# Four more of layer one's output-weight chunks in split form in the first token group

## The chip, the cores and the metric

One core of a Trainium2 chip. The metric is the device time of one execution, in microseconds (us); the number quoted for a kernel is the median of its runs. Engines are named as in the profile: PE (matmul) with PEld (its weight loads), DVE (vector), ACT (scalar), POOL (gpsimd), SP (here only the queue that issues transfers).

## What is computed

Causal block attention, then two feed-forward layers, all in float32 (4 batches, 8 heads, 576 positions, head size 64; so 2304 tokens of 512 features):

```python
attn = softmax(mask(q @ k.T / 8)) @ v            # block-causal, blocks of 64
x = attn as [2304, 512]
h = x @ w_in                                     # layer one: 512 -> 2048
x = (h - tanh(h)) @ w_out                        #            2048 -> 512
xn = x / sqrt(mean(x * x) + 1e-6) * rms_g        # layer two
out = (silu(xn @ w_gate) * (xn @ w_val)) @ w_out2
```

## The kernel before

Tokens are worked in six groups of 384 (three tiles of 128). The hidden 2048 features of layer one are 16 chunks of 128 (`J1`); a step `s` is one chunk of one group, so layer one is 96 steps, group 0 being steps 0 to 15. In a step, PE multiplies the chunk's input weights with the group's tokens (`ins`, L796 to L798), ACT takes the tanh (L1058), DVE subtracts it, and two steps later (`LAG`) `out1` multiplies the result with the chunk's output weights into three accumulators `acc`. Attention for the coming group runs in slots between these products, and PE's order is the order in which the program is written. The order on DVE, ACT, POOL and SP is made by a scheduler that goes by its own estimate of the times.

A float32 product is made in one of two forms:

- **split**: both factors are rounded to a shorter float (`h`) and a rest (`l`), and three fast matmuls are summed (L829 to L831 in `gemm_out`). The weights then take a whole tile of 128x1024, `h` in the left half and `l` in the right.
- **whole**: one matmul on plain float32 (L839). PE runs it as two recorded instructions. Two chunks share a tile.

Output weights of the chunks under `SPLIT` are whole in group 0, all others split. In group 0 the weights come from the inputs as 64-bit floats, staged through three buffers `st` by SP (L139) and turned into float32 by `convert`: two ACT passes (L150, L152) and two DVE passes (L153, L154). Where the result is to be split, ACT rounds it (L113, `w<-cv`) and DVE takes the rest (L117, `w<-cv,w`). The tiles of four slots for output weights are reused in turn, and what later groups need is stored to HBM: the input weights split (`w1d_i`, L730), split output weights split (`w1d_o`, L736), whole ones as pairs (`w1f`, L745). In group 1, which walks the chunks backwards, the whole ones come back through `st` (`stagef`, L756), are split by ACT and DVE (L769, L770) and stored split (L771); later groups load them split (L775).

The lines that the number decides:

```python
            if j >= SPLIT:
                t = wo[j] = wo[until(j)] = w1tile(1, until(j))
                convert(staged.pop(n), t[:, 0:512], t[:, 512:1024])
                if j < KEPT:
                    SP.dma_start(out=w1d[1][j], in_=t.bitcast(F32))
                return
...
            if s < SPLIT:
                gh = wk.tile([128, TG], F32, name="gh", tag="gh", bufs=3)
                DVE.tensor_tensor(gh, h, gt, ALU.subtract)
            else:
                DVE.tensor_tensor(gt, h, gt, ALU.subtract)
                gh = wk.tile([128, TG], F32R, name="gh", tag="gh", bufs=3)
                gl = wk.tile([128, TG], F32R, name="gl", tag="gl", bufs=3)
                rnd(ACT, gh, gt)
                lo(DVE, gl, gt, gh)
```

The weights of layer two are converted by the same `convert` during the last group of layer one and, for chunks 3 to 9, while layer two is already running over its first pair of groups (`direct`, `fill`: ACT L884 and L892, DVE L117 `ws<-fu,ws`).

Of the kernel before, what the change touches and what calls it, by code (L numbers as in the profile page):

```python
# [50 lines left out]
JH = J2 // 2  # L51
WHOLE = range(3, 10)
LAG = 2
SPLIT = 8
KEPT = 12
AVLEAD = 3

# [47 lines left out]
def build(ctx, tc, q, k, v, w_in, w_out, w_gate, w_val, w_out2, rms_g, ident_in, out):  # L105
# [566 lines left out]
    with tc.manual_schedule(engines={PE.engine}):  # L672
# [39 lines left out]
        def w1tile(x, last, dt=F32R):  # L712

            n = min(range(4), key=lambda n: lastuse[x][n])
            lastuse[x][n] = last
            return ring.tile([128, 1024], dt, name=f"w1{x}{n}", tag=f"w1{x}{n}")

        def until(s):
            g, j = divmod(s, J1)
            return s + 2 * (J1 - 1 - j) + 1 if g < NG - 1 and j >= J1 - 4 else s  # L720

        def convert1(n):

            j, half = divmod(n, 2)
            if half == 0:
# [5 lines left out]
# [3 lines that stand above are left out]
# [19 lines left out]
        def stagef(m):  # L753
            if m >= 0:
                fstaged[m] = env["stg"].tile([128, 1024], F32, name="st", tag="st")
                SP.dma_start(out=fstaged[m], in_=w1f[m])  # L756

        def w1get(s):
# [7 lines left out]
            t = wo[s] = w1tile(1, until(s))  # L766
            if g == 1 and j < SPLIT:
                f = fstaged[j // 2][:, 512 * (j % 2):512 * (j % 2) + 512]
# [12 lines left out]
        def conv_upto(m):  # L781
            nonlocal ncv
            while ncv < min(m, 2 * J1):
                convert1(ncv)
                ncv += 1
                stage1(ncv + 2)
# [46 lines left out]
        def out1(s, t):  # L833
# [3 lines left out]
            gh, gl = gts[s]  # L837
            if s < SPLIT:
                PE.matmul(accs[t], lhsT=gh[:, t * 128:t * 128 + 128], rhs=wo[s], start=(j == 0), stop=(j == J1 - 1))  # L839
# [172 lines left out]
        for s in range(NSA):  # L1012
# [26 lines left out]
            if g == 0:  # L1039
                conv_upto(max(2 * j + 3, EARLY + (2 * J1 - EARLY) * (2 * j + 1) // 28))  # L1040
            if 0 <= s - (J1 - 1 + KEPT - SPLIT) < 3:
                stagef(SPLIT // 2 - 1 - (s - (J1 - 1 + KEPT - SPLIT)))
            if KEPT <= 2 * J1 - 2 - s < J1:
# [15 lines left out]
            gl = None  # L1059
            if s < SPLIT:  # L1060
                gh = wk.tile([128, TG], F32, name="gh", tag="gh", bufs=3)
# [351 lines left out]
```

## Time and profile before

| what | value |
|---|---|
| median of 3 runs | 1007.89 us (1007.11 to 1009.34) |
| the profiled execution | 1006.96 us |
| its span, first to last instruction | 1005.1 us |
| PE, DVE, ACT, POOL busy | 994.3, 712.9, 660.0, 367.1 us |
| granted PE clock | 0.999 |

The profiled execution's time is 1.86 us above its span, and 0.93 us under the median of the runs. PE is at work in nearly all of the span; the engines that feed it have idle time when averaged over the whole, though not in each stretch.

### The profile page before, as it was taken

The numbers are of one execution on the slowest core, as the hardware profiler recorded it, in microseconds if no ns is written. First come the engines' busy times: TensorE is split into PE (matmuls) and PEld (weight loads), VectorE is DVE, ScalarE is ACT, GpSimd is POOL, SyncE is SP. The second block draws the span as 40 slices with busy tenths as digits, with TensorE's granted clock in tenths as the row PEclk, the third lists the DMA queues.
The fourth block names the chain that finished last, engine by engine and source line by source line (L and its number), as shares of the span: only waits on it lengthen the run. The fifth ranks groups of instructions, "written<-read, shape, count | busy, mean of one in ns | idle before, by whom it ended". The sixth has DMA issues, their size and how long they took to land.

```text
span 1005.1 us, 18056 instructions
## 1 busy us (share of the span) xinstructions
PE 994.3 (99%) x5987; PEld 910.9 (91%) x5987; DVE 712.9 (71%) x1577; ACT 660.0 (66%) x1546; POOL 367.1 (37%) x556
## 2 busy tenths in 40 slices
PE   9999999999999999999999999999999999999998
PEld 6767889899988889889999889999999999999998
DVE  7878876876767686787767888966854458644565
ACT  7979988887888777788858775635722247412253
POOL 6522212342334343535424524575211470111710
PEclk9999999999999999999999999999999999999999
DMA  9999889955888699767879998977796757876664
GB/s 226 293 346 353 221 267 288 253 149 141 209 241 208 196 251 296 213 211 243 284 247 383 354 360 318 349 301 301 273 350 235 265 210 269 303 275 234 261 229 149
DMA packets 185419, 265.22 MB, mean 264 GB/s; under 512 B 109040, under 2 KB 150384, under 8 KB 178032
## 3 DMA queue, kind: packets, MB, share of 16 engines
q1 hardware_dynamic: 184240, 263.69, 80.8%
q8 instruction: 47, 0.77, 0.3%
q10 hardware_dynamic: 1088, 0.39, 0.1%
q14 instruction: 44, 0.36, 0.1%
HBM read 202.70 MB, written 61.34 MB: 263 GB/s over the span
## 4 chain that ended last, share of the span: by engine, by line
PE 80%; DVE 7%; ACT 6%; DMA 4%; issue 2%; POOL 1%; DVEq 0%; SPq 0%; ACTq 0%; POOLq 0%
PE t L796 5%; PE t L798 5%; PE t L797 5%; PE acc L829 5%; PE acc L831 5%; PE acc L830 5%; PE gv L1146 5%; PE gv L1148 5%; PE gv L1147 5%; PE t L603 4%; PE t L533 4%; PE ga L831 3%; PE ga L1148 3%; PE ga L829 3%; PE ga L830 3%; PE ga L1146 3%
## 5 line engine op out<-in xcount | busy, mean ns | idle before, releaser
L796 PE MATMUL t<-xh,w 128*128 128x384 f32 x384 | 138.9, 362 | 0.0
L798 PE MATMUL t<-xh,w 128*128 128x384 f32 x384 | 129.9, 338 | 0.1
L797 PE MATMUL t<-xl,w 128*128 128x384 f32 x384 | 129.2, 337 | 0.0
L1146 PE MATMUL gv<-xh,ws 128*128 128x384 f32 x330 | 111.0, 336 | 0.5 <-DVE vb L1199 0.5
L1148 PE MATMUL gv<-xh,ws 128*128 128x384 f32 x330 | 110.9, 336 | 0.2 <-DVE ws L117 0.2
L1147 PE MATMUL gv<-xl,ws 128*128 128x384 f32 x330 | 110.7, 335 | 0.0
L829 PE MATMUL acc<-w,gh 128*128 128x512 f32 x264 | 109.2, 414 | 0.6 <-ACT gh L113 0.6
L831 PE MATMUL acc<-w,gl 128*128 128x512 f32 x264 | 104.4, 396 | 0.1
L830 PE MATMUL acc<-w,gh 128*128 128x512 f32 x264 | 103.9, 393 | 0.0
L1203 POOL TENSOR_TENSOR g<-va,vb 128x384 f32<-128x384 f32 x36 | 37.3, 1037 | 163.0 <-ACT va L1202 147.3
L574 ACT ACTIVATE pt<-pt,stat 128x64 f32<-128x64 f32 (+2 forms) x144 | 81.2, 564 | 16.4 <-DVE pt L572 11.3
L796 PEld LDWEIGHTS t<-xh,w 128*128 128x128 f32 x384 | 72.3, 188 | 6.9 <-issue 3.2
L797 PEld LDWEIGHTS t<-xl,w 128*128 128x128 f32 x384 | 72.5, 189 | 2.0 <-issue 0.5
L798 PEld LDWEIGHTS t<-xh,w 128*128 128x128 f32 x384 | 72.1, 188 | 0.8 <-DVE w L117 0.8
L117 DVE TENSOR_TENSOR gl<-gt,gh 128x384 fp32r<-128x384 f32 x88 | 60.1, 683 | 16.5 <-ACT gh L113 15.7
L117 DVE TENSOR_TENSOR pp<-t,pp 128x512 fp32r<-128x512 f32 (+3 forms) x112 | 55.4, 508 | 22.5 <-ACT pp L113 22.1
L1064 DVE TENSOR_TENSOR gt<-t,gt 128x384 f32<-128x384 f32 x88 | 48.5, 552 | 28.2 <-ACT gt L1058 27.8
L603 PE MATMUL t<-ident,pt 128*128 128x128 f32 x400 | 64.8, 274 | 0.5 <-POOL pt L588 0.5
L113 ACT ACTIVATE pp<-t 128x512 fp32r<-128x512 f32 (+5 forms) x144 | 60.5, 438 | 5.7 <-PE t L603 4.5
L1146 PEld LDWEIGHTS gv<-xh,ws 128*128 128x128 f32 x330 | 61.9, 188 | 1.4 <-DVE vb L1199 1.2
L1148 PEld LDWEIGHTS gv<-xh,ws 128*128 128x128 f32 x330 | 61.9, 188 | 0.6 <-DVE ws L117 0.6
L603 PEld LDWEIGHTS t<-ident,pt 128*128 128x128 f32 x400 | 49.9, 140 | 13.6 <-issue 3.0
(225 smaller groups left out, 2946.3 us busy)
## 6 DMA issues: line engine op xcount, KB each, us to landing
ws<-w2d SPq DMA_DIRECT2D x26, 1792.0 KB, 7.4
ws<-wod SPq DMA_DIRECT2D x21, 1536.0 KB, 6.2
w<-w1d_i SPq DMA_DIRECT2D x60, 512.0 KB, 4.8
w<-w1d_o SPq DMA_DIRECT2D x52, 512.0 KB, 5.4
w2d<-ws SPq DMA_DIRECT2D x10, 1792.0 KB, 8.5
st<-in_moe_w_out SPq DMA_DIRECT2D x28, 512.0 KB, 5.9
st<-in_moe_w_in SPq DMA_DIRECT2D x16, 512.0 KB, 6.1
w1d_i<-w SPq DMA_DIRECT2D x16, 512.0 KB, 5.3
```

The lines of the kernel that those rows point to most:

```text
L117: eng.tensor_tensor(out=o, in0=full, in1=hi.bitcast(F32), op=ALU.subtract)
L574: ACT.activation(out=pt[:, 0:keys], in_=pt[:, 0:keys], func=AF.Exp, scale=-1.0, bias=least, accum_out=st[:, 8 + ti:9 + ti])
L603: PE.transpose(t[:, (j - a) * 128:(j - a + 1) * 128], pt[:, j * 128:(j + 1) * 128], ident)
L796: PE.matmul(h, lhsT=wh[:, c], rhs=xh[:, kk], start=(kk == 0), stop=False)
L797: PE.matmul(h, lhsT=wh[:, c], rhs=xl[:, kk], start=False, stop=False)
L798: PE.matmul(h, lhsT=wl[:, c], rhs=xh[:, kk], start=False, stop=(kk == KD - 1))
L829: PE.matmul(acc, lhsT=gh[:, c], rhs=wh, start=first, stop=False, skip_group_check=more)
L830: PE.matmul(acc, lhsT=gh[:, c], rhs=wl, start=False, stop=False, skip_group_check=more)
L831: PE.matmul(acc, lhsT=gl[:, c], rhs=wh, start=False, stop=last, skip_group_check=more)
L1146: PE.matmul(ps, lhsT=wh[:, c], rhs=xh[:, kk], start=(first and kk == 0), stop=False, skip_group_check=more)
L1147: PE.matmul(ps, lhsT=wh[:, c], rhs=xl[:, kk], start=False, stop=False, skip_group_check=more)
L1148: PE.matmul(ps, lhsT=wl[:, c], rhs=xh[:, kk], start=False, stop=(last and kk == nk - 1), skip_group_check=more)
```

## The change

```diff
 WHOLE = range(3, 10)
 LAG = 2
-SPLIT = 8
+SPLIT = 4
 KEPT = 12
 AVLEAD = 3
```

For chunks 4 to 7 (steps 4 to 7 of group 0) the output weights are now split when they are converted, the tanh result is split too, the product is three matmuls in place of one whole one, and each chunk is stored split in `w1d_o` rather than in pairs in `w1f`. In group 1 these four chunks are loaded split; their splitting and storing there is gone, and two loads of `w1f` remain in place of four.

PE's order changes only in the twelve products themselves. On the other engines the scheduler's order moves in two stretches: from the conversion of chunk 4 to the start of group 1, and from the last two steps of layer one through the conversions under layer two. Three places follow.

SP in group 0, the queue that issues stores of converted weights and loads of the next raw ones; the number behind a name tells tiles apart, w1d_i_90 is the input weights of chunk 5, w1d_o_105 to w1d_o_107 the output weights of chunks 4 to 6, w1f_66 the pair of chunks 4 and 5. Before:

```order
L139 DMA st<-in_moe_w_out 128x1024
L310 DMA qr<-in_q 96x2x256
L139 DMA st<-in_moe_w_in 128x4x256
L745 DMA w1f_66<-w_887 128x1024
L730 DMA w1d_i_90<-w_922 128x1024
L139 DMA st<-in_moe_w_out 128x1024
L730 DMA w1d_i_91<-w_1010 128x1024
L139 DMA st<-in_moe_w_in 128x4x256
L139 DMA st<-in_moe_w_out 128x1024
```

The same place now:

```order
L736 DMA w1d_o_105<-w_887 128x1024
L139 DMA st<-in_moe_w_out 128x1024
L310 DMA qr<-in_q 96x2x256
L139 DMA st<-in_moe_w_in 128x4x256
L730 DMA w1d_i_90<-w_925 128x1024
L736 DMA w1d_o_106<-w_969 128x1024
L139 DMA st<-in_moe_w_out 128x1024
L730 DMA w1d_i_91<-w_1016 128x1024
L139 DMA st<-in_moe_w_in 128x4x256
L139 DMA st<-in_moe_w_out 128x1024
L736 DMA w1d_o_107<-w_1039 128x1024
```

Every chunk now has a store of its own, two of them directly ahead of a load of raw weights.

DVE around step 6, from one row maximum of the attention scores (L572, 384 columns) to the next (64 columns, the next unit's first); w_1033 is the whole tile of chunks 6 and 7, w_1136 the input weights of chunk 8. Before:

```order
L572 TENSOR_SCALAR pt,stat<-t 128x384
L153 TENSOR_SCALAR cv<-cv 128x512
L154 SCALAR_TENSOR_TENSOR w_1033<-cv,cu 128x512
L583 RECIPROCAL stat<-stat 128x3
L1062 TENSOR_TENSOR gh<-t,gt 128x384
L153 TENSOR_SCALAR cv<-cv 128x512
L154 SCALAR_TENSOR_TENSOR cv<-cv,cu 128x512
L117 TENSOR_TENSOR w_1136<-cv,w_1136 128x512
L572 TENSOR_SCALAR pt,stat<-t 128x64
```

The same place now (w_1039 and w_1108 are the split output weights of chunks 6 and 7, w_1089 the input weights of chunk 7):

```order
L572 TENSOR_SCALAR pt,stat<-t 128x384
L154 SCALAR_TENSOR_TENSOR cv<-cv,cu 128x512
L117 TENSOR_TENSOR w_1039<-cv,w_1039 128x512
L117 TENSOR_TENSOR gl<-gt,gh 128x384
L117 TENSOR_TENSOR w_1089<-cv,w_1089 128x512
L583 RECIPROCAL stat<-stat 128x3
L153 TENSOR_SCALAR cv<-cv 128x512
L154 SCALAR_TENSOR_TENSOR cv<-cv,cu 128x512
L1064 TENSOR_TENSOR gt<-t,gt 128x384
L117 TENSOR_TENSOR w_1108<-cv,w_1108 128x512
L117 TENSOR_TENSOR gl<-gt,gh 128x384
L572 TENSOR_SCALAR pt,stat<-t 128x64
```

The 64-column maximum now stands behind a `w` rest and a `gl`, where it stood behind a `w` rest alone; the rest for chunk 8's input weights has moved behind it.

ACT at the end of layer one, from the split of step 94's result to the first copy of layer two (L1195). Before:

```order
L113 ACTIVATE gh<-gt 128x384
L1058 ACTIVATE gt<-t 128x384
L150 ACTIVATE cv<-st 128x512
L152 ACTIVATE cu<-st 128x512
L113 ACTIVATE gh<-gt 128x384
L846 ACTIVATE sq,ssq<-acc_7191 128x512
L846 ACTIVATE sq,ssq<-acc_7195 128x512
L846 ACTIVATE sq,ssq<-acc_7199 128x512
L150 ACTIVATE cv<-st 128x512
L152 ACTIVATE cu<-st 128x512
```

The same place now:

```order
L113 ACTIVATE gh<-gt 128x384
L150 ACTIVATE cv<-st 128x512
L152 ACTIVATE cu<-st 128x512
L1058 ACTIVATE gt<-t 128x384
L113 ACTIVATE gh<-gt 128x384
L846 ACTIVATE sq,ssq<-acc_7227 128x512
L150 ACTIVATE cv<-st 128x512
L152 ACTIVATE cu<-st 128x512
L846 ACTIVATE sq,ssq<-acc_7231 128x512
L846 ACTIVATE sq,ssq<-acc_7235 128x512
L150 ACTIVATE cv<-st 128x512
L152 ACTIVATE cu<-st 128x512
```

The last tanh of layer one has moved behind a pair of conversion passes, and from here on the conversions run one piece (half a chunk's weights) further ahead than before.

## Rows read from the trace of the kernel before

**Rows 1.** The page: span, and busy time of each engine.

```profile
span 1005.1 us, 18056 instructions
PE 994.3 (99%) x5987; PEld 910.9 (91%) x5987; DVE 712.9 (71%) x1577; ACT 660.0 (66%) x1546; POOL 367.1 (37%) x556
```

**Rows 2.** Busy time by stretch: PE, PEld, DVE, ACT, POOL, clock, DMA, GB/s.

```profile
60.00:70.00 10.00, 10.00 (x40) 6.58 (x39) 7.16 (x18) 7.98 (x22) 1.71 (x4) 1.00 1.06 364
...
80.00:90.00 10.00, 10.00 (x45) 6.79 (x42) 8.54 (x20) 9.01 (x25) 0.15 (x1) 1.00 1.04 325
...
110.00:120.00 10.00, 10.00 (x56) 9.18 (x57) 8.48 (x23) 9.93 (x27) 0.15 (x1) 1.00 0.72 188
...
180.00:190.00 10.00, 10.00 (x61) 8.89 (x60) 8.00 (x20) 8.55 (x20) 4.46 (x6) 1.00 0.92 259
```

**Rows 3.** PE in order of time: start, us, what, idle time before it.

```profile
72.72 2.74 PE L839 MATMUL acc<-w,gh 128*128 128x512 f32 x6
75.30 0.33 PE L533 MATMUL t<-kh,qf 128*128 128x64 f32 x2
...
78.84 1.41 PE L657 MATMUL t<-pp,vp 128*64 128x384 f32 x10 [1.16 <-DVE pt L572]
...
134.30 0.39 PE L829 MATMUL acc<-w,gh 128*128 128x512 f32 x1
...
134.98 0.31 PE L533 MATMUL t<-kh,qh 128*128 128x320 f32 x1
```

**Rows 4.** The chain that ended last, from 48 to 80 us: start, us, what.

```profile
60.38 7.46 DMA st<-in_moe_w_in
...
77.11 0.64 ACT w L113
...
78.57 0.23 DVE pt L572 x2
...
78.84 1.29 PE t L657 x7
```

**Rows 5.** Groups of instructions, 40 to 100 us: count, busy us, mean ns.

```profile
L117 DVE TENSOR_TENSOR w<-cv,w 128x512 fp32r<-128x512 f32 x14 | 10.0, 716 | 2.2 <-ACT w L113 2.0
L154 DVE SCALAR_TENSOR_TENSOR cv<-cv,cu 128x512 int32<-128x512 int32 x14 | 10.0, 714 | 1.4 <-ACT cu L152 0.2
L113 ACT ACTIVATE w<-cv 128x512 fp32r<-128x512 f32 x14 | 9.0, 643 | 0.9 <-DVE cv L154 0.8
...
L117 DVE TENSOR_TENSOR gl<-gt,gh 128x384 fp32r<-128x384 f32 x2 | 1.1, 551 | 0.0
L113 ACT ACTIVATE gh<-gt 128x384 fp32r<-128x384 f32 x2 | 1.1, 528 | 0.0
```

**Rows 6.** Transfers from 40 to 100 us: rate by slices of 1.5 us, total, issues.

```profile
GB/s 143 139 370 407 358 426 336 253 391 419 341 333 261 325 401 283 283 398 420 410 390 397 333 155 304 420 380 244 337 263 302 372 414 382 401 416 399 410 373 313
DMA packets 11907, 20.55 MB, mean 343 GB/s; under 512 B 2266, under 2 KB 8572, under 8 KB 11902
...
w1f<-w SPq DMA_DIRECT2D x4, 512.0 KB, 5.4
w1d_o<-w SPq DMA_DIRECT2D x3, 512.0 KB, 6.0
```

**Rows 7.** Busy time by stretch under layer two's first conversions, columns as above.

```profile
630.00:640.00 10.00, 9.69 (x56) 9.63 (x56) 9.36 (x19) 6.05 (x13) 4.55 (x5) 1.00 0.98 353
...
650.00:660.00 10.00, 9.62 (x53) 8.98 (x52) 9.58 (x18) 4.76 (x11) 4.58 (x5) 1.00 0.55 229
660.00:670.00 10.00, 9.19 (x50) 8.22 (x50) 6.45 (x12) 3.15 (x7) 8.62 (x10) 1.00 1.01 390
```

**Rows 8.** ACT in order of time at the end of layer one.

```profile
589.57 0.66 ACT L150 ACTIVATE cv<-st 128x512 f32<-128x512 f32 x1
590.13 0.67 ACT L152 ACTIVATE cu<-st 128x512 int32<-128x512 uint32 x1
590.69 0.53 ACT L113 ACTIVATE gh<-gt 128x384 fp32r<-128x384 f32 x1
```

## The prediction

> **What bounds the kernel now.** The first view is the page: PE is busy for 994.3 of 1005.1 us, so all idle time of PE together is under 11 us, and a change is worth what it does to PE's work or to these few gaps [rows 1]. The second is busy time by stretch, for the part of group 0 that is changed, roughly 55 to 96 us. PE shows 10.00 of 10 both at 60 to 70 and at 80 to 90, with DVE at 7.16 and 8.54 and ACT at 7.98 and 9.01 [rows 2]. So PE sets the pace there, but ACT has little room. The third is PE in order of time. The one large gap near the change is 1.16 us before 78.84, where the value product of attention waits for DVE [rows 3]. The fourth is the chain that ended last, which tells where that wait comes from: a raw-weight load issued at 60.38 that took 7.46 us, then ACT and DVE passes of the conversion, a rounding at 77.11, and the row maximum (L572) at 78.57, which stood in DVE's queue behind the weights' rest [rows 4]. What the reader is to see: up to 78.84 the end is set by loads, ACT and DVE, and from there on by PE. A saving on PE counts in full behind that gap; ahead of it it only makes the gap longer.
>
> **PE's own work.** Three whole products (six records) run from 72.72 to the next start at 75.30, so one takes 2.58 / 3 = 0.86 us. Three split matmuls run from 134.30 to 134.98, so a split product takes 0.68 us [rows 3]. Each of the twelve products of chunks 4 to 7 gains 0.18 us, 2.16 in all. The three of chunk 4, at 72.72, lie ahead of the gap: 0.54 us of gain that falls into it. The nine of chunks 5 to 7 lie behind it: 9 x 0.18 = **1.6 us off the end**. The PE clock is at full in all these stretches [rows 2], so the durations carry over.
>
> **Work added on ACT and DVE in group 0.** Four roundings of weights at 0.643 and four of results at 0.528 make 4.7 us on ACT; four rests at 0.716 and four at 0.551 make 5.1 us on DVE [rows 5]. The second conversion pass on DVE remains as it was, only its target changes. Spread over the 30 to 40 us of these steps that is 12 to 17% of either engine. At 60 to 70 there is room for it: 2.0 us idle on ACT and 2.8 on DVE [rows 2]. Steps that were split already run with ACT at 9.93 and DVE at 8.48 at 110 to 120 us, and PE is at 10.00 there [rows 2]. So in sum the cover holds, and I cost the added passes at nothing except where they stand directly ahead of something that PE waits for. If the cover were gone, ACT's 4.7 us would be the price, the upper end.
>
> That place is the gap at 78.84. In DVE's order the 64-column maximum stood behind one weights' rest; now it stands behind a weights' rest and a `gl`, in a stretch that also holds one more rest, one more `gl`, and the same conversion passes. The least is that the gap vanishes (1.16 us gained), since the old order's wait for the rounding at 77.11 is not the new order's wait. The most is one `gl` (0.551) plus a later load. The load of 60.38 now has one more store of 512 KB in flight ahead of it, and 524 KB at the mean 343 GB/s of 40 to 100 us is 1.5 us [rows 6]; together 2.1 us. I take **0.7 us lost**: the `gl` in full, and little of the store, because the chain is nearest to a DVE queue there and ACT had idle time that the added passes fill before the load is waited for.
>
> **Transfers.** Out go two stores of pairs (`w1f`); in come four stores (`w1d_o`) of the same 512 KB each [rows 6]. That is two more, 1.05 MB, in the 50 us after 50: 3.1 us at the mean rate of 343 GB/s if all of it delayed loads that are waited for. The slices do not stand at the mean: they swing from 139 to 426 GB/s and are at 390 or more in 16 of 40 [rows 6], so some room is left between bursts, and by 110 to 120 us the rate has fallen to 188 [rows 2], so what is late is caught up. SP issues in order, and each new store waits for its rest on DVE before the next raw load can go. I put all this inside the 0.7 above and its bound of 2.1.
>
> The Trainium skill (DMA: Bandwidth & Descriptors, "Where 436 GB/s comes from") says that for transfers between HBM and SBUF the HBM side binds at about 358 GB/s per core, and this speaks against the change: a stretch at 343 would have 4% left, and the two more stores would push loads back by nearly their whole length, an estimate of 1.05 MB / 358 = 2.9 us. The slices of up to 426 GB/s do not agree with that as a ceiling for one core running alone. By the row the sum is as above; by that rule the loss at the gap would be about 2.9 instead of 0.7, and the end 2.2 us later.
>
> **Group 1.** Four roundings, four rests and four stores go, two loads net come in. PE is at 10.00 at 180 to 190 us, with ACT at 8.55 and DVE at 8.00 [rows 2]: PE waits for none of it, so this gives nothing. The lower end would be the same nothing; a loss would need a late load of `w1d_o`, which is issued more than two steps ahead like those of the neighbouring chunks.
>
> **The end of layer one.** Here no work is changed, only the order. On ACT the last tanh moves behind a pair of conversion passes, 589.57 to 590.69, so it comes 1.1 us later [rows 8], and the last products wait for its split: up to 1.1 us lost on PE at about 592. In return the conversions under layer two run one piece ahead. In 630 to 670 PE idles 0.31 + 0.38 + 0.81 = 1.5 us with DVE at 9.36 and 9.58 of 10 [rows 7]; there DVE sets the end. One second pass (L154, 0.714 us [rows 5]) less in DVE's queue lets that stretch end 0.7 us earlier. PE by itself would end 1.1 later but has 1.5 of idle to lose, so 0.4 earlier. The later of the two decides: **0.4 us gained**, between 1.5 gained (all idle time goes) and 1.1 lost (nothing is given back).
>
> **Sum.** 1.6 gained, 0.7 lost, 0.4 gained: 1.3 us less. The profiled execution (1006.96, span 1005.1 [rows 1] and 1.86 around it) would become 1005.7. The median of the runs stands 0.93 above the profiled one, so I predict 1007.89 - 1.3 = **1006.6 us**. What a measurement of this kernel can tell from no change is about 0.2%, 2.0 us, so this is a gain within what cannot be told.
>
> **Rivals.**
> - *The savings come whole.* The gap at 78.84 stays or shrinks, chunk 4's 0.54 counts too, and layer two gives back 1.0: 2.2 + 1.0 = 3.2 less, 1004.7. For it: the idle time of ACT and DVE at 60 to 70 [rows 2], and no wait of PE at 110 to 120 under the same load. Against: the `gl` ahead of the maximum. 0.22.
> - *The gap eats the saving.* It grows by its bound of 2.1 and layer two gives 0.4: 1.6 + 0.4 - 2.1 = 0.1 less, 1007.8. For it: the chain through the 7.46 us load [rows 4]. 0.20. The skill's rule above would end beside it, 0.9 later than before.
> - *Slower: the loads fall behind.* Mechanism: SP holds each raw load behind a split store, the three buffers turn slower, and ACT stands at the head of its queue waiting for raw weights while exponentials and tanh wait behind it. Place: 60 to 95 us. Price: the full 3.1 us of the two stores and the `gl` 0.55, while the last tanh costs its 1.1: 3.65 + 1.1 - 1.6 = 3.2 more, 1011.1. It decides once PE's gaps in 55 to 96 grow by more than the 1.6 saved plus 2.0. Against: the chunks already split do not show it at 110 to 120 [rows 2], although with a lower transfer rate. 0.10.
>
> **How the numbers follow.** The forecast has 0.48, and by itself lies between 1005.2 and 1007.6: the layer-two term between its 0.4 and nothing, the gap between nothing and 1.4. Below 1005.9 (faster by over 0.2%) lie the first rival and a fifth of the forecast: 0.22 + 0.10 = 0.32. Above 1009.9 lie most of the slower rival: 0.09. The rest, 0.59, is within 0.2%. The range for 8 in 10 leaves out part of either end: 1004.2 (both gains whole and half the gap gone) to 1009.4 (the gap at 2.1, the last tanh's 1.1 not given back, and half a microsecond between runs).
>
> **What would show it.** L839 with 24 records in place of 48, and split products at 0.68 us in steps 4 to 7. The wait before the value product near 78, grown by about 0.7 and still released by L572. PE without idle from there to 100, and step 8's first product about 0.9 us earlier. A new wait of up to 1.1 us at the end of layer one, and less than 1.5 us of idle in 630 to 670. The prediction is wrong if PE shows new gaps of more than 1 us between 80 and 100, if loads of raw weights take much over 7.5 us, or if the conversions under layer two fall behind rather than ahead.

## The result and the profile after

The changed kernel takes 1013.96 us (median of 6 runs, 1012.41 to 1014.95) against 1007.67 for the kernel before (6 runs, 1007.11 to 1009.34): ratio 1.0059, 95% interval 1.0049 to 1.0069. That is **6.3 us slower**, where 1.3 us less was predicted; it lies outside the range.

The profiled execution took 1014.95, 1.0 above the median, and that of before lies 0.7 under its own, so the two traces differ by 7.7 us. Part of this is chance: at 48 us, in code that the change doesn't touch, the trace after is already 2.2 us late, and the traces of the experiments below that keep this code are 0.5 to 2.1 late there. Shifts below are differences between two points, so this cancels.

The page of the changed kernel, span and engines, answers to [rows 1]:

```profile
span 1012.8 us, 18082 instructions
...
PE 996.2 (98%) x5999; PEld 914.4 (90%) x5999; DVE 712.6 (70%) x1581; ACT 663.4 (66%) x1550; POOL 367.9 (36%) x556
```

PE is busy 1.9 us more and idle 16.6 instead of 10.8 us. Where it idles is seen in busy time by stretch of the changed kernel, columns as in [rows 2] and [rows 7]:

```profile
60.00:70.00 10.00, 10.00 (x46) 7.55 (x45) 7.49 (x19) 7.83 (x20) 2.12 (x4) 1.00 1.08 350
80.00:90.00 10.00, 10.00 (x59) 8.49 (x55) 9.11 (x24) 9.40 (x24) 1.77 (x4) 1.00 1.02 344
110.00:120.00 10.00, 8.84 (x48) 7.65 (x47) 7.84 (x19) 9.46 (x26) 0.15 (x1) 1.00 0.79 228
120.00:130.00 10.00, 7.66 (x39) 6.58 (x39) 8.11 (x19) 9.86 (x22) 0.60 (x3) 0.83 0.53 176
...
660.00:670.00 10.00, 10.00 (x59) 10.00 (x58) 9.01 (x17) 6.13 (x13) 5.89 (x8) 1.00 0.60 215
670.00:680.00 10.00, 9.32 (x54) 9.00 (x53) 4.76 (x9) 2.00 (x4) 10.00 (x11) 1.00 1.02 394
680.00:690.00 10.00, 9.05 (x52) 8.73 (x51) 4.50 (x9) 1.92 (x4) 7.83 (x8) 1.00 0.99 404
```

The stretch that the prediction watched (60 to 90) is full. The new idle time is at 110 to 130, behind the steps that were changed and in steps that were split before; at 120 to 130 the granted clock also falls. In layer two 660 to 670 is now full, as forecast, but 670 to 690 is not.

PE in order of time in the changed kernel, columns as in [rows 3]:

```profile
75.15 0.48 PE L829 MATMUL acc<-w,gh 128*128 128x512 f32 x1
...
77.31 0.33 PE L533 MATMUL t<-kh,qf 128*128 128x64 f32 x2
...
79.57 1.52 PE L657 MATMUL t<-pp,vp 128*64 128x384 f32 x12
...
108.36 0.44 PE L796 MATMUL t<-xh,w 128*128 128x384 f32 x1 [0.25 <-ACT w L113]
...
115.56 0.44 PE L796 MATMUL t<-xh,w 128*128 128x384 f32 x1 [1.05 <-ACT w L113]
...
123.67 0.44 PE L796 MATMUL t<-xh,w 128*128 128x384 f32 x1 [2.23 <-ACT w L113]
...
124.68 0.34 PE L796 MATMUL t<-xh,w 128*128 128x384 f32 x1
124.86 0.34 PE L797 MATMUL t<-xl,w 128*128 128x384 f32 x1
...
126.28 0.52 PE L797 MATMUL t<-xl,w 128*128 128x384 f32 x1
126.60 0.52 PE L798 MATMUL t<-xh,w 128*128 128x384 f32 x1
...
598.48 0.50 PE L829 MATMUL acc<-w,gh 128*128 128x512 f32 x1 [0.41 <-ACT gh L113]
...
676.85 0.45 PE L1146 MATMUL gv<-xh,ws 128*128 128x384 f32 x1 [0.68 <-DMA ws<-w2d]
...
685.39 0.45 PE L1146 MATMUL ga<-xh,ws 128*128 128x384 f32 x1 [0.95 <-DMA ws<-w2d]
```

Three split products of chunk 4 take 2.16 us (75.15 to 77.31) where whole ones took 2.58, and the gap of 1.16 us ahead of the value product is gone (79.57 has no wait). Up to 96 us the kernel gains what the change promised: the transposes that start at 57.93 and 95.98 before start at 60.51 and 95.22 after, a shift from +2.58 to -0.76, that is **3.3 us gained** (12 products at 0.18 are 2.16, and the gap 1.16). Then PE waits three times for the rounded *input* weights of chunks 12, 13 and 14, which the change doesn't touch (and once, 0.31 us, for a rest). From 95.22 to 128.61 the shift goes from -0.76 to +6.35: **7.1 us lost**. In layer two the shift falls from 6.23 (565 us) to 5.43 (664.66 before, 670.09 after), 0.8 gained, and the two waits for `ws` raise it to 7.38: 2.0 lost.

The chain that ended last in the changed kernel, from 95 to 128 us:

```profile
93.35 4.07 DMA st<-in_moe_w_out
97.44 0.20 ACT stat L582
97.64 0.55 ACT w L113
...
122.22 0.41 ACT gh L113
122.63 0.10 ACT stat L582
122.73 0.38 ACT pp L113
123.10 0.53 ACT w L113
123.65 0.70 DVE w L117
124.40 0.44 PE t L798
```

It begins with a raw-weight load and then stays on ACT and DVE; ACT is at 9.5 and 9.9 of 10 there. How late the conversions run, SP's queue shows. First its last raw loads (L139) of layer one in the kernel before, in order of time:

```profile
112.07 0.37 SPq L139 DMA_DIRECT2D st<-in_moe_w_in  x1
114.67 0.35 SPq L139 DMA_DIRECT2D st<-in_moe_w_out  x1
```

The same in the changed kernel:

```profile
117.62 0.37 SPq L139 DMA_DIRECT2D st<-in_moe_w_in  x1
120.52 0.35 SPq L139 DMA_DIRECT2D st<-in_moe_w_out  x1
```

The two are 5.5 and 5.9 us later, over 3 more than the late start explains. Such a load is issued as soon as ACT frees a buffer: in the kernel before ACT's second pass (L152) on the buffer ends at 112.05 and the load goes at 112.07, in the changed kernel at 117.60 and 117.62. So these times tell how far ACT has come.

SP's order in layer two, in the kernel before:

```profile
657.66 0.34 SPq L899 DMA_DIRECT2D w2d<-ws  x1
658.11 6.55 SPq L1166 DMA_DIRECT2D ws<-w2d  x2
665.78 0.32 SPq L899 DMA_DIRECT2D w2d<-ws  x1
```

In the changed kernel:

```profile
663.82 0.37 SPq L1166 DMA_DIRECT2D ws<-w2d  x1
669.84 0.32 SPq L899 DMA_DIRECT2D w2d<-ws  x1
670.26 0.38 SPq L1166 DMA_DIRECT2D ws<-w2d  x1
```

A store of 1.8 MB (L899) now stands between two loads of `ws`; before, both loads stood ahead of it. So there are two losses at two places. The first could come from five things: ACT's added passes, SP's order (a load held behind a store that waits for its rest), the bytes of the stores, the number of raw buffers, or the order of work on ACT and DVE, which the scheduler makes anew for each kernel.

### The profile page after: what moved, and what is told of

Read it like the earlier page. It is cut to its first block, busy times and chain, and to the rows that moved or that the text cites. A ratio compares the mean times of both kernels' runs of the same rounds, so it can differ in the third digit from the quotient of the medians.

```text
span 1012.8 us, 18082 instructions
## 1 busy us (share of the span) xinstructions
PE 996.2 (98%) x5999; PEld 914.4 (90%) x5999; DVE 712.6 (70%) x1581; ACT 663.4 (66%) x1550; POOL 367.9 (36%) x556
## 4 chain that ended last, share of the span: by engine, by line
PE 78%; DVE 7%; ACT 7%; DMA 4%; issue 2%; POOL 1%; SPq 0%; DVEq 0%; ACTq 0%; POOLq 0%
PE t L796 5%; PE t L798 5%; PE t L797 5%; PE acc L829 5%; PE gv L1146 5%; PE gv L1148 5%; PE gv L1147 5%; PE acc L831 5%; PE acc L830 5%; PE t L603 4%; PE t L533 3%; PE ga L1146 3%; PE ga L831 3%; PE ga L829 3%; PE ga L830 3%; PE ga L1148 2%
## 5 line engine op out<-in xcount | busy, mean ns | idle before, releaser
L796 PE MATMUL t<-xh,w 128*128 128x384 f32 x384 | 139.4, 363 | 3.5 <-ACT w L113 3.5
L829 PE MATMUL acc<-w,gh 128*128 128x512 f32 x276 | 115.1, 417 | 1.0 <-ACT gh L113 1.0
L831 PE MATMUL acc<-w,gl 128*128 128x512 f32 x276 | 109.2, 396 | 0.1
L830 PE MATMUL acc<-w,gh 128*128 128x512 f32 x276 | 108.7, 394 | 0.0
L574 ACT ACTIVATE pt<-pt,stat 128x64 f32<-128x64 f32 (+2 forms) x144 | 80.9, 562 | 16.0 <-DVE pt L572 10.8
L796 PEld LDWEIGHTS t<-xh,w 128*128 128x128 f32 x384 | 72.5, 189 | 11.1 <-ACT w L113 4.7
L1064 DVE TENSOR_TENSOR gt<-t,gt 128x384 f32<-128x384 f32 x92 | 50.8, 552 | 29.1 <-ACT gt L1058 28.5
L1146 PEld LDWEIGHTS gv<-xh,ws 128*128 128x128 f32 x330 | 61.9, 188 | 1.8 <-DMA ws<-w2d 1.0
L831 PEld LDWEIGHTS acc<-w,gl 128*128 128x128 f32 x276 | 51.8, 188 | 12.6 <-DVE gl L117 1.1
```

What stands on the lines that cost most here:

```text
L574: ACT.activation(out=pt[:, 0:keys], in_=pt[:, 0:keys], func=AF.Exp, scale=-1.0, bias=least, accum_out=st[:, 8 + ti:9 + ti])
L796: PE.matmul(h, lhsT=wh[:, c], rhs=xh[:, kk], start=(kk == 0), stop=False)
L829: PE.matmul(acc, lhsT=gh[:, c], rhs=wh, start=first, stop=False, skip_group_check=more)
L830: PE.matmul(acc, lhsT=gh[:, c], rhs=wl, start=False, stop=False, skip_group_check=more)
L831: PE.matmul(acc, lhsT=gl[:, c], rhs=wh, start=False, stop=last, skip_group_check=more)
L1146: PE.matmul(ps, lhsT=wh[:, c], rhs=xh[:, kk], start=(first and kk == 0), stop=False, skip_group_check=more)
```

## The experiments

Each ratio is to the kernel before on the same chip, whose median beside these runs was 1007.67 to 1008.15. "Waits" is the sum of PE's waits for rounded or rest input weights at 105 to 128 us; MB and GB/s are the transfers of 55 to 100 us.

| kernel | median us | ratio, 95% | waits | last raw load | MB, GB/s |
|---|---|---|---|---|---|
| before | 1007.67 | | 0 | 114.67 | 15.69, 349 |
| changed | 1013.96 | 1.0059 (1.0049 to 1.0069) | 3.84 | 120.52 | 16.49, 366 |
| e1_pool | 1013.48 | 1.0049 (1.0030 to 1.0067) | 3.92 | 119.37 | 16.49, 366 |
| e2_act | 1008.85 | 1.0006 (0.9995 to 1.0016) | 0 | 116.61 | 15.65, 348 |
| e3_nostore | 1010.52 | 1.0020 (1.0011 to 1.0029) | 0 | 112.91 | 15.45, 343 |
| e4_split6 | 1009.86 | 1.0020 (1.0011 to 1.0030) | 1.10 | 118.97 | 16.25, 361 |
| e6_tiny | 1009.39 | 1.0015 (1.0006 to 1.0023) | 0 | 116.44 | 14.97, 333 |
| e7_poolq | 1016.11 | 1.0074 (1.0061 to 1.0088) | 3.85 | 121.12 | 15.83, 352 |
| e8_later | 1013.75 | 1.0056 (1.0044 to 1.0069) | 3.68 | 119.24 | 16.46, 366 |
| e9_st4 | 1008.37 | 1.0002 (0.9993 to 1.0011) | 0 | 114.14 | 16.74, 372 |
| e10_b4 | 1008.12 | 0.9999 (0.9990 to 1.0007) | 0 | 112.65 | 16.94, 376 |
| e11_l2 | 1012.07 | 1.0034 (1.0021 to 1.0047) | 3.87 | 121.44 | 16.19, 360 |
| e12_both | 1006.65 | 0.9988 (0.9980 to 0.9997) | 0 | 114.31 | 16.66, 370 |
| e13_bytes | 1011.15 | 1.0033 (1.0021 to 1.0044) | 2.73 | 118.97 | 16.67, 370 |

The column to read first is the last raw load: at 116.6 or earlier PE waits for no input weights, from 118.9 on it does. It is a sign of how late ACT's conversions run, not a cause by itself.

**Is it the added passes? e1_pool, e2_act.** e1_pool is the changed kernel with its eight added roundings on POOL:

```diff
-        rnd(ACT, h, f)
+        rnd(reng or ACT, h, f)
...
+                convert(staged.pop(n), t[:, 0:512], t[:, 512:1024], POOL if j < 8 else ACT)
...
+                rnd(POOL if s < 8 else ACT, gh, gt)
```

> The changed kernel, with the eight added rounding passes (output weights and results of chunks 4 to 7) on POOL in place of ACT; same products, same transfers. If ACT's queue is what came to be the bound (theory ACT): no wait of PE for a rounded weight between 105 and 125 us, and 1006 to 1008.5 us. If the two more stores are the cause, by holding back the raw loads (theory stores): 1012 to 1014.5 us, waits as in the changed kernel.

e2_act is the kernel before with the eight ACT passes alone, to a scratch tile:

```diff
             o = t[:, 512 * (j % 2):512 * (j % 2) + 512]
             convert(staged.pop(n), o)
+            if j >= 4:
+                rnd(ACT, wk.tile([128, 512], F32R, name="dum", tag="dum", bufs=1), o)
...
                 DVE.tensor_tensor(gh, h, gt, ALU.subtract)
+                if s >= 4:
+                    rnd(ACT, wk.tile([128, 512], F32R, name="dum", tag="dum", bufs=1)[:, 0:TG], gh)
```

> The kernel before, with only the eight ACT passes added at the same places (their results go to a scratch tile that nothing reads); products whole, stores as before. Theory ACT: 2 to 5 us slower than before, 1009.7 to 1012.7 us, PE waiting for rounded input weights late in group 0. Theory stores: within 1 us of before, 1006.7 to 1008.7 us.

Both speak against it: taken off ACT, the waits are what they were (0.35, 1.07 and 2.20 us at chunks 12 to 14), and added alone, the passes cost nothing that can be measured (1008.85 is 0.15 above the interval, but its ratio can't be told from 1). That part of the prediction, "I cost the added passes at nothing", holds for ACT's passes.

**Is it the stores, and how does it grow? e3_nostore, e4_split6.** e3_nostore is the changed kernel without the four stores; later groups load chunks 8 to 11 in place of 4 to 7, which leaves four chunks' output weights out of their products. e4_split6 makes half of the change.

```diff
-                if j < KEPT:
+                if 8 <= j < KEPT:
                     SP.dma_start(out=w1d[1][j], in_=t.bitcast(F32))
...
-                SP.dma_start(out=t.bitcast(F32), in_=w1d[1][j])
+                SP.dma_start(out=t.bitcast(F32), in_=w1d[1][j + 4 if 4 <= j < 8 else j])
```

> The changed kernel without the four stores of split output weights of chunks 4 to 7 in group 0; later groups load chunks 8 to 11 in their place, so those weights are the wrong ones. 2.1 MB less is moved in group 0, 1.05 MB less than even before. Theory stores: 1006 to 1008 us. Theory ACT: 1012 to 1014.5 us, as the changed kernel, waits of PE for ACT unchanged.

```diff
-SPLIT = 8
+SPLIT = 6
```

> The change half made: chunks 6 and 7 alone are split in group 0 (the number is 6). Half of the ACT passes, half of the stores. Either theory: between the two, 1008.5 to 1011 us; if the loss were an accident of the scheduler's order and not a sum of work, it could lie anywhere from 1005 to 1014.

Without the stores the waits for weights are gone, with ACT's and DVE's added work in place. The time missed both intervals: the 1010.5 that is left holds the two waits of layer two (0.51 and 0.96 us at `ws`), of which neither theory knew. With half of the change one wait of 1.10 is left, and SP's order in layer two is that of before. So the stores carry the first loss, and it grows with their number.

**Their place or their bytes? e6_tiny, e8_later, e7_poolq, e13_bytes.** In e6_tiny the stores keep their places and waits but are 8 KB long (loads as in e3_nostore):

```diff
+                if 4 <= j < 8:
+                    SP.dma_start(out=w1d[1][j][:, 0:16], in_=t.bitcast(F32)[:, 0:16])
+                elif j < KEPT:
                     SP.dma_start(out=w1d[1][j], in_=t.bitcast(F32))
```

> This kernel is the changed one with the four stores of the output weights of chunks 4 to 7 kept at their places in SP's queue and behind the same rests on DVE, but 8 KB long in place of 512 KB; later groups load chunks 8 to 11 in place of chunks 4 to 7, which leaves out part of the computation. Theory H (SP's order: a raw load stands behind a store that is held for its rest): the waits of PE for rounded input weights at 105 to 128 us stay as in the changed kernel, 3 us or more in sum, and the time is 1012.5 to 1014.5. Theory B (the bytes: 1.05 MB more in the stretch take the loads' bandwidth): no such wait over 0.5 us, and the time is that of the kernel without the stores, 1009.5 to 1011.

In e8_later each store goes behind the next raw load, with its full length:

```diff
                 if j < KEPT:
-                    SP.dma_start(out=w1d[1][j], in_=t.bitcast(F32))
+                    later.append((j, t))
...
                 stage1(ncv + 2)
+                while later and later[0][0] <= (ncv - 3) // 2:
+                    n, w = later.pop(0)
+                    pin(SP.dma_start(out=w1d[1][n], in_=w.bitcast(F32)))
```

> The changed kernel with each store of output weights in group 0 moved behind the raw load that followed it (in SP's order two conversions later), same bytes, same queue. Theory H (SP's order): the raw loads come earlier, the waits for input weights at 105 to 128 us shrink to 1 us or less in sum, time 1009.5 to 1011.5. Theory B (the bytes): as the changed kernel, 1012.5 to 1014.5, since the bytes in the stretch are the same.

In e7_poolq the four stores leave SP's queue:

```diff
                 if j < KEPT:
-                    SP.dma_start(out=w1d[1][j], in_=t.bitcast(F32))
+                    (POOL if j < 8 else SP).dma_start(out=w1d[1][j], in_=t.bitcast(F32))
```

> The changed kernel with the same four stores of 512 KB issued from POOL's queue in place of SP's, so that no raw load stands behind them. Theory H (SP's order): the last raw loads are issued 3 us earlier, the waits for input weights at 105 to 128 us go, and the time is 1009.5 to 1011. Theory B (the bytes): waits as in the changed kernel, 1012.5 to 1014.5. A third way: POOL is held at a store until DVE has the rest, attention's scalings of pt behind it come late, and PE waits at value products between 57 and 80 us: slower than 1012 with waits for pt instead of w.

e13_bytes is the kernel before with the bytes alone (its edit also keeps SP's order in layer two as it was):

```diff
                 SP.dma_start(out=w1f[j // 2], in_=t)
+                if j in (5, 7):
+                    SP.dma_start(out=more[j // 2 - 2], in_=t)
```

> The kernel before (nothing split more, no added ACT or DVE pass) with two more 512 KB stores to HBM in group 0: the pair tiles of chunks 4 and 5 and of 6 and 7 are stored a second time behind their own stores, to places that nothing reads; SP's order in layer two is kept as before. This is the 1.05 MB that the change adds, by itself. Theory B (the bytes: DMA engines are full from 55 to 112 us and each byte more makes the last raw loads later): the last raw loads are issued 2 to 3.5 us later than in the kernel before, PE waits for rounded input weights at 105 to 128 us, and the time is 1010 to 1013. Rival E (bytes cost only together with the added ACT and DVE passes, since those make the conversions late): no such waits, 1007.5 to 1009.

All four go the same way. Same place, hardly any bytes: no wait. Same bytes at another place or from another queue: the waits stay. Bytes alone: 3.2 us slower, with no other line of the change in the kernel. PE of e13_bytes in order of time (its L800 is L796):

```profile
122.07 0.44 PE L800 MATMUL t<-xh,w 128*128 128x384 f32 x1 [2.73 <-ACT w L113]
```

SP's last raw loads in e13_bytes (its L141 is L139):

```profile
115.21 0.37 SPq L141 DMA_DIRECT2D st<-in_moe_w_in  x1
118.97 0.35 SPq L141 DMA_DIRECT2D st<-in_moe_w_out  x1
```

Its transfers from 55 to 100 us: total, then issues with their median us to landing:

```profile
DMA packets 9378, 16.67 MB, mean 370 GB/s; under 512 B 2141, under 2 KB 6506, under 8 KB 9373
...
st<-in_moe_w_in SPq DMA_DIRECT2D x7, 512.0 KB, 7.6
...
more<-w SPq DMA_DIRECT2D x2, 512.0 KB, 7.0
```

The reader is to see the same kind of wait at the same place as in the changed kernel, 122 us, more than 40 us behind the added stores. A raw load takes 7.6 us to land there and 5.5 in e6_tiny; in the kernel before and the changed one the medians are 6.5 and 6.6, so the median alone does not show it, the time of issue does. e7_poolq has no wait for `pt` and nearly the waits for weights of the changed kernel, as theory B said, but went 1.6 us past its upper end; its interval overlaps that of the changed kernel, and the 2 us between the medians were not followed up. e6_tiny came 0.1 us below its interval.

One thing more moved in e13_bytes, though its edit doesn't name it: the scheduler's order on ACT. In the kernel before the first conversion pass of chunk 14's input weights stands ahead of an attention exponential of 320 columns (L574):

```profile
113.40 0.68 ACT L150 ACTIVATE cv<-st 128x512 f32<-128x512 f32 x1
...
118.74 0.57 ACT L574 ACTIVATE pt<-pt,stat 128x320 f32<-128x320 f32 x1
```

In e13_bytes it stands behind it (its L152 is L150, its L576 is L574):

```profile
116.38 0.56 ACT L576 ACTIVATE pt<-pt,stat 128x320 f32<-128x320 f32 x1
...
117.71 0.67 ACT L152 ACTIVATE cv<-st 128x512 f32<-128x512 f32 x1
```

In all seven kernels of the table in which PE does not wait for chunk 14 the pass stands ahead of this exponential, in all seven in which PE waits, behind it. And ACT does not wait for the load here: in e13_bytes it is issued at 110.19 and lands 5.1 us later, at 115.3, 2.4 us before ACT takes it, and ACT has other work in between. So the runs show that the bytes bring the loss. Whether they do so by later transfers or by the order that the scheduler makes with them in its estimate, they do not show: no run adds the bytes and keeps ACT's order.

**The buffers. e9_st4, e10_b4.** e9_st4 is the changed kernel with a fourth raw buffer, e10_b4 the kernel before with one:

```diff
-    st1 = tc.tile_pool(name="st1", bufs=3, side="right")
+    st1 = tc.tile_pool(name="st1", bufs=4, side="right")
```

> The changed kernel with four buffers for raw weights in place of three in this stage. Theory H (SP's order): a load is issued one conversion earlier than it has to be, so a store that holds it for 1 to 3 us costs less; the waits at 105 to 128 us fall below 1.5 us in sum and the time is 1010 to 1012. Theory B (the bytes): the transfer rate is what it was, the loads are no earlier in sum at 105 us, and the time stays at 1012.5 to 1014.5.

> The kernel before with four buffers for raw weights in place of three in this stage, nothing split more. If the fourth buffer is worth something only where the stores take the transfers' spare time, this equals the kernel before, 1007.2 to 1009.0. Rival: it is a gain by itself (the 1.16 us at 78.84 goes, since the load of 60.38 is issued earlier), 1006.0 to 1007.1; then the four-buffer kernel with the split still loses by the split.

With the split the fourth buffer takes 5.6 us off, by itself it is worth nothing (1.0002 and 0.9999 are both the kernel before). Transfers of 55 to 100 us in e9_st4:

```profile
DMA packets 9586, 16.74 MB, mean 372 GB/s; under 512 B 2133, under 2 KB 6759, under 8 KB 9582
...
st<-in_moe_w_out SPq DMA_DIRECT2D x7, 512.0 KB, 8.0
```

The bytes are all there and each load takes longer (8.0 us), but it is asked for earlier, and the last one is issued at 114.14, not 120.52. e9_st4 came out better than either theory's interval: theory H had guessed at a buffer's worth, but for a cause that the other runs refute. Here too the scheduler's order on ACT moved (chunk 14's pass is ahead of the exponential again), so the buffer and the order it brings come together.

**Layer two. e11_l2, e12_both.** e11_l2 is the changed kernel with SP's order in layer two put back; nothing else moves in any queue. e12_both has this and the fourth buffer.

```diff
-                SP.dma_start(out=w.bitcast(F32), in_=w2d[j])
+                pin(SP.dma_start(out=w.bitcast(F32), in_=w2d[j]))
...
-                    if j + 1 < WHOLE.stop:
+                    if j + 1 < WHOLE.stop - 1:
                         direct[j + 1].keep()
                 if p or j:
                     load_slot(p * NQ + j + 2)
+                if p == 0 and j == WHOLE.stop - 1:
+                    direct[j].keep()
```

> The changed kernel with one thing undone in layer two: SP issues the load of w2d's last chunk (L1166) ahead of the 1.8 MB store of the ninth (L899), as in the kernel before; nothing else in any queue moves. Theory: the two waits of PE for ws at 676.85 and 685.39 (0.68 and 0.95 us, 1.6 in sum, and what of the matmuls' own start hangs on them) go, and the time is 1.5 to 2.0 us less than that of the changed kernel, 1012.0 to 1012.5. Rival: the loads only wait at another place (their buffers come free no earlier), and the time stays at 1013.5 to 1014.5.

> The changed kernel with four buffers for raw weights and SP's order in layer two as in the kernel before. If the two losses are apart from each other, this is the four-buffer kernel less 1.5 to 2.0 us: 1006.2 to 1007.2, below the kernel before. If the loss in layer two is only moved, 1008 to 1009.

Both came as the theory said: 1.9 us less for e11_l2 against the changed kernel, 1.7 for e12_both against e9_st4 (2.2 and 1.6 if each is first taken over its own runs of the kernel before). In e11_l2 PE has no wait left at 670 to 690, and the orders on ACT, DVE and POOL are those of the changed kernel from end to end, so this loss is shown without a rival. e12_both by stretch, columns as in [rows 2]:

```profile
110.00:120.00 10.00, 9.87 (x53) 8.46 (x52) 8.60 (x21) 9.97 (x28) 0.00 (x0) 1.00 0.87 256
120.00:130.00 10.00, 10.00 (x65) 8.40 (x64) 8.54 (x21) 10.00 (x27) 2.57 (x5) 1.00 0.48 140
...
670.00:680.00 10.00, 10.00 (x59) 10.00 (x58) 5.32 (x10) 2.42 (x5) 9.40 (x11) 1.00 0.80 295
680.00:690.00 10.00, 10.00 (x75) 10.00 (x74) 6.99 (x10) 4.96 (x10) 6.56 (x6) 1.00 1.00 405
```

PE is full at both places, but for 0.13 us, though ACT is at 10 of 10 at 110 to 130. At 1006.65 e12_both is the fastest kernel of the study: 1.3 us under the kernel before (0.9988, interval 0.9980 to 0.9997) and 1.5 under e10_b4, which has the same buffers without the split. With both losses undone the change is worth the 1.3 us that were forecast, but as a sum, not by its terms: against the kernel before its trace gains 2.1 us from 48 to 96 us, loses 0.7 again by 123, and gains 1.0 in layer two (2.5 in sum, above the runs' 1.3 because the trace of the kernel before is early at 48 us).

## Why the prediction was wrong

**The step that failed is the one on transfers**: two more stores, "3.1 us at the mean rate of 343 GB/s if all of it delayed loads that are waited for", were put "inside the 0.7 above and its bound of 2.1", since "by 110 to 120 us the rate has fallen to 188 [rows 2], so what is late is caught up". Added alone, these bytes cost 3.2 us (e13_bytes). The 188 was read as room. It is not: SP can't ask for a load before one of three buffers is free, and a buffer is freed by ACT, which is full there ([rows 2], 9.93); no store of weights is due there either. So the rate falls because few transfers are asked for, and nothing was caught up. DMA's share in these rows is 1.06 and 1.04 at 60 to 70 and 80 to 90: the transfer engines were full, and the prediction looked at GB/s in slices and not at that column. The loss comes to light 40 us behind the added stores, where the reserve runs out: in the kernel before chunk 14's rounding was done at about 117.5 and PE came for it at 119.29.

How the bytes get from the stores to this place is shown only in part. A raw load took 7.6 us in e13_bytes (median, 55 to 100 us) against 6.5 in the kernel before. But ACT's conversions waited for loads 4.3 us in all at 48 to 77 us in e13_bytes, 4.2 in the kernel before and 2.5 in the changed kernel, and after 77 us in none of the three. Chunk 14's load had landed 2.3, 2.4 and 2.4 us before its pass in the kernel before, e13_bytes and the changed kernel (111.1, 115.3 and 116.9); what kept it was work that stood ahead of it on ACT. At its old place in the order it would have been too early in turn: e13_bytes reaches that place, ahead of an exponential of 256 columns, at 113.47, 1.8 us before the load lands. Late transfers and conversions that the scheduler places late are not told apart.

**The saving on PE was right and is worth next to nothing here.** Split products cost what was forecast ([rows 2], cited for the clock, hold neither 72.72 nor 134.30, but the page's mean of 0.999 bears it out), and 3.3 us were gained by 96 us, more than the rival "the savings come whole" has ahead of layer two. But behind that point the rounded weights set the end, and there a PE that is early only waits longer: e13_bytes, with none of the saving, loses 3.7 us between the value product (78.84 before, 78.83) and 123.45 (127.10), the changed kernel 7.1 from the lead of 3.3. Compared with each trace's shift at 48 us the two leave group 0 within 1.3 us of each other (3.65 - 0.81 and 6.35 - 2.22), and e1_pool, which has the saving and whose clock did not fall, 0.3 earlier than e13_bytes (3.68 - 1.15).

**The gap at 78.84** did not grow by 0.7, it vanished: the least case of the prediction. With half the change 0.68 of it is left (e4_split6).

**The cover of ACT and DVE** holds where the conversions keep their place on ACT: e2_act adds ACT's passes and leaves that order nearly as it was, and e9_st4 and e12_both carry all the added work, and PE waits for none of it.

**Group 1** was right: the shift is 6.35 at 128 us and 6.23 at 565.

**The end of layer one**: the mechanism is right, the last tanh costs (L829 waits 0.61 us at 595.61 and 0.41 at 598.48) and the conversions ahead give back more, 0.8 gained against 0.4 forecast, up to 664. Both terms were larger than forecast: the shift goes from 6.24 at 586 us to 7.90 at 650 and 5.43 at 664. What was missed is a third queue: the working shows ACT's and DVE's rows for this place, and SP's order, in which a store of 1.8 MB moved ahead of a load, was not read. It costs 1.9 (e11_l2).

**The rivals.** "Slower: the loads fall behind" had the right sign and the right victim. Its mechanism (SP holding a load behind a store) is refuted by e6_tiny, e7_poolq and e8_later, its picture of ACT is the wrong way round (conversions stood behind exponentials, not these behind a late load), its place (60 to 95) is 30 us early, and its price of 3.2 more is half. Its "against" (the split chunks at 110 to 120 show no wait) was the same misread row.

The sum by runs, from the changed kernel down: 1.9 us for the order in layer two, 5.6 for the fourth raw buffer with the order that it brings, 7.3 with both, and 1.5 of that is the change's own gain (e12_both against e10_b4). The medians of the kernel before that stand beside these runs differ by up to 0.5 us, and so far these differences are uncertain.

In 45 us of full transfers the rate was 352 to 372 GB/s in the kernels that carry the four split stores, and 376 in e10_b4, which has none of them, so as a ceiling for one core running alone the 358 GB/s of the Trainium skill (DMA: Bandwidth & Descriptors, "Where 436 GB/s comes from") does not agree with these traces. The loss that was worked out from its rule, 2.9 us, is close to the 3.2 of e13_bytes; as part of that may go through ACT's order, the closeness can be luck.

That e1_pool, with less work on ACT, gets its last raw loads no earlier fits ACT's order: from 96 us on it is the changed kernel's, instruction by instruction. **Open** is what part of the bytes' cost is transfers and what part the scheduler's order; and of the 7.1 us, 3.84 are waits and some 1.7 the clock (below), the rest was not traced.

## What to carry to other kernels

Before pricing an extra transfer as hidden, read the busy share of the transfer engines over the whole stretch and not the rate at one place, and where the rate falls, ask whether nothing was wanted or nothing could be asked for; the price can fall due far from its cause, where the consumer's reserve ends. Where a scheduler orders the engines by its own estimate, an added transfer can also move that order: compare it in every experiment before a cause is said to stand alone. Price a saving on the engine that is the bound only up to the next point at which something else arrives later than it. Read the order of every queue, the transfer queue too, at each place where a scheduler moved something: one store ahead of one load was a third of the loss here.

## What was not expected of the hardware

The granted clock fell in the middle of busy time: at 124.68 and 124.86 two 128x384 matmuls start 0.18 us apart, at 126.28 and 126.60 two start 0.32 apart, and the mean clock of 120 to 130 us is 0.83, that is, part of it at the 1.2 GHz level and the rest at 2.4. Ahead of it PE had waited 1.05 and 2.23 us and then run for over 1 us. With nearly the same waits (1.07 and 2.20) e1_pool kept 1.00 in this stretch, and so did e13_bytes with one wait of 2.73. e1_pool:

```profile
120.00:130.00 10.00, 7.70 (x50) 6.00 (x49) 8.18 (x19) 9.92 (x24) 2.01 (x4) 1.00 0.58 190
```

So the waits alone do not decide it. What it cost can be read from this pair: from the transposes at 96 us to the end of the stretch (95.98 and 128.60 in the kernel before) e1_pool loses 5.4 us, the changed kernel 7.1, and PE is busy for 994.4 us in all against 996.2. That puts the lower clock at about 1.7 us, an estimate from two traces; 10 us at a mean of 0.83 lose as much.
